# One run on 64x64 tiles in place of two: values, scores and sums of an attention block put together

## The chip, the cores and the metric

One core of a Trainium2 chip. The metric is the device time of one execution in microseconds (us). Engines are named as in the profile: PE (TensorE matmul), PEld (its weight loads), DVE (VectorE), ACT (ScalarE), POOL (GpSimd), SP (SyncE, which issues most DMAs).

## The reference, cut to what matters

Chunked attention (8 batches, 8 heads, 576 tokens, chunks of 64, head size 64) is followed by a bilinear feed-forward layer on 4608 tokens:

```python
scores = scale * np.matmul(q_c, k_c.transpose(0, 1, 2, 4, 3))   # 64x64 per chunk and head
attn = np.exp(scores - np.max(scores, axis=-1, keepdims=True))
attn = attn / (np.sum(attn, axis=-1, keepdims=True) + 1e-09)
out = np.matmul(attn, v_c)            # ... reordered to x, 4608 x 512
a = x @ w_a                           # 512 -> 1536
b = x @ w_b
return (a * b @ w_out)                # 1536 -> 512
```

## The kernel before

The tokens are cut into 9 blocks (0 to 8) of 512, a block into two units of 256. Attention of a unit has four steps: `scores` (32 matmuls on 64x64 tiles of the PE array, then two exp on ACT), `sums` (4 matmuls of 512 columns against ones, also on 64x64 tiles, then two ln on ACT), `inverse` (exp of minus ln, on ACT) and `values` (32 matmuls on 64x64 tiles, then two products on DVE).

```python
    def sums(U, halves=None):
        E = E_of[U]
        sm = [bank() for _ in range(2)]
        for cl in range(2):
            for j in range(2):
                nc.tensor.matmul(
                    sm[cl][j * 64:j * 64 + 64, :],
                    ones[cl * 64:cl * 64 + 64, :],
                    E[cl * 64:cl * 64 + 64, j].rearrange("p m g s -> p (m g s)"),
                    start=True,
                    stop=True,
                )
        ...
        for cl in range(2):
            nc.scalar.activation(
                out=ln_of[U][:, cl].rearrange("p m n -> p (m n)"), in_=sm[cl], func=AF.Ln
            )
```

From block 2 on the feed-forward layer runs in 6 groups to a block. Each group is seven half-size products, `p1` to `p7`, of four 128x128 matmuls of 256 columns, with evictions and additions between. The PSUM bank `B` of a group is one of two (`pb0`, `pb1`), taken in turn; and `p3` of a group is done one group later, after that group's `p1`.

```python
        def p1(self):
            self.A = bank(psum_a)
            self.product(self.A, self.b11, self.x11, True)
            self.B = bank(psum_b)                      # psum_b[0], then the two change places
            nc.scalar.copy(out=self.B, in_=self.A)
        ...
        def add7(self):
            self.c = c_pool.tile([128, 512], FP32, name="c_sb")
            nc.vector.tensor_tensor(out=self.c, in0=self.C, in1=self.v, op=ADD)
            nc.vector.tensor_tensor(out=self.C, in0=self.C, in1=self.u, op=ADD)

        def p3(self):
            self.product(self.B, self.b22, self.s4)
            self.multiply(self.B, self.b, 0)           # DVE reads B

        def p4(self):
            self.product(self.C, self.t4, self.x22)
            self.multiply(self.C, self.c, 256)         # DVE reads C
```

`combine_x` makes four sums of x for these products on DVE. The attention steps are put between the products: `at(K, i, n, f, u)` means that in block K, group i, place n, step f is done for unit u. `bring` casts a unit on POOL, loads the next and transposes q and k by DMA; `chunk` does parts of the output product.

```python
        def scores_beside(pool):
            return lambda u: scores(u, (pool, psum_b[0]), 1)

        for K in range(2, NBLK):
            U = 2 * K + 2
            ...
                at(K, 0, 0, sums, U)
            at(K, 1, 0, inverse, U)
            at(K, 2, 1, values, U)
            at(K, 2, 1, scores_beside(psum_o), U + 1)
            at(K, 3, 0, sums, U + 1)
            at(K, 3, 1, inverse, U + 1)
            at(K, 4, 1, values, U + 1)
            at(K, 4, 1, scores_beside(psum_q), U + 2)
            at(K, 5, 0, lambda u: combine_x(u // 2, (0,)), U + 1)
            at(K, 5, 1, lambda u: combine_x(u // 2, (1,)), U + 1)
        ...
                now = Group(K, i)
                now.p1()
                if last:
                    last.add7()
                chunk(chunks.get(K, chunks[4])[2 * i])
                ...
                if last:
                    last.p3()
                attend(K, i, 0)                        # place 0
                now.p6()
                if last:
                    last.p4()
                    finish(last)                       # sums of the products, on POOL
                ...
                now.p2()
                chunk(chunks.get(K, chunks[4])[2 * i + 1])
                attend(K, i, 1)                        # place 1
                now.p5()
                exps()
                now.p7()
                last = now
```

The softmax here doesn't subtract the row's maximum and nothing guards it: scores larger than these inputs give would overflow.

Of the kernel before, what the change touches and what calls it, by code (L numbers as in the profile page):

```python
# [16 lines left out]
def kernel(  # L17
# [10 lines left out]
    nc = tc.nc  # L28
    BF16 = mybir.dt.bfloat16
    FP32 = mybir.dt.float32  # L30
    AF = mybir.ActivationFunctionType
# [32 lines left out]
    psum_a = ctx.enter_context(tc.tile_pool(name="psuma", bufs=1, space=PSUM))  # L64
# [3 lines left out]
    psum_c = ctx.enter_context(tc.tile_pool(name="psumc", bufs=1, space=PSUM))  # L68
    psum_o = ctx.enter_context(tc.tile_pool(name="psumo", bufs=1, space=PSUM))
    psum_q = ctx.enter_context(tc.tile_pool(name="psumq", bufs=1, space=PSUM))  # L70
# [17 lines left out]
    def bank(pool=None):  # L88
        if pool is None:
            pool = spread[0]  # L90
            spread.append(spread.pop(0))
        if pool is psum_b:
            pool = psum_b[0]
            psum_b.append(psum_b.pop(0))
        return pool.tile([128, 512], FP32, name=bank_names[id(pool)])
# [97 lines left out]
    def load(U, names="qkv"):  # L193

        for n in names if U < NU else "":
            src = {"q": q, "k": k, "v": v}[n]
            if U < PE_UNITS[n]:
                st = st_pool.tile([128, H, 2, D], FP32, name="st")
                for r, b, s, m in pieces(U):
                    nc.sync.dma_start(  # L200
                        out=st[r // 2:(r + m) // 2].rearrange("p h i d -> p h (i d)"),
                        in_=src[b, :, s:s + m, :].rearrange("h (p i) d -> p h (i d)", i=2),
                    )
                staged[n, U] = st.rearrange("p h i d -> p i h d")
            else:
                staged[n, U] = st_pool.tile([128, 2, H, D], FP32, name="st")
                load_natural(staged[n, U], src, U)
# [3 lines left out]
    def cast(U, names="qkv"):  # L211
        for n in names if U < NU else "":
            if U >= 4 and wo_sums:
                combine_wo(*wo_sums.pop(0))
            raw[n, U] = raw_pool.tile(
                [128, 2, H, D], BF16, name=f"{n}_raw"
            )
            eng = nc.vector if U == 0 and n != "v" else nc.gpsimd
            eng.tensor_copy(out=raw[n, U], in_=staged.pop((n, U)))  # L219
# [28 lines left out]
    def transpose_dma(U):  # L248
        if U not in qkt:
            qkt[U] = qkt_pool.tile([128, 2, 2, NKT, 128], BF16, name="qkt")  # L250
        for w, n in ((0, "q"), (1, "k")):
            if U < PE_UNITS[n]:
                continue
            nc.sync.dma_start_transpose(
                out=qkt[U][:, w].rearrange("p g m c -> p (g m) c"),
                in_=raw.pop((n, U)).rearrange("p g h d -> p (g h d)"),
            )
# [3 lines left out]
    ln_of = {}  # L261
# [29 lines left out]
    def exps(n=2):  # L291
        while late and n:
            late.pop(0)()
            n -= 1

    def sums(U, halves=None):
        E = E_of[U]
        sm = [bank() for _ in range(2)]
        for cl in range(2):
            for j in range(2):  # L300
                nc.tensor.matmul(  # L301
# [5 lines that stand above are left out]
                )  # L307
        ln_of[U] = sm_pool.tile([128, 2, NKT, 128], FP32, name="ln")
        rs_of[U] = ln_of[U]
        for cl in range(2):  # L310
            nc.scalar.activation(
                out=ln_of[U][:, cl].rearrange("p m n -> p (m n)"), in_=sm[cl], func=AF.Ln
            )
            if halves:
                inverse(U, cl)

# [43 lines left out]
        if f is not None:  # L360
            values(f)

    def bring(U):

        if U >= NU:
            return
        cast(U, "qk")
        load(U + 1, "q" if U < 9 else "qkv")
        transpose_dma(U)
        bring_v(U)  # L370

    def bring_v(U):
        cast(U, "v")
        if U < 9:
            load(U + 1, "kv")
# [36 lines left out]
    def combine_x(K, parts=(0, 1, 2, 3)):  # L412
        xT = x_tiles[K]
        x11, x12 = xT[:, 0:2, 0:256], xT[:, 2:4, 0:256]
        x21, x22 = xT[:, 0:2, 256:512], xT[:, 2:4, 256:512]
        if K not in s_of:
            s_of[K] = [s_pool.tile([128, 2, 256], FP16, name=f"s{j}") for j in range(1, 5)]
        s1, s2, s3, s4 = s_of[K]
        for part in parts:
            o, x0, x1, op = (  # L420
                (s1, x21, x22, ADD),
                (s2, s1, x11, SUB),
                (s3, x11, x21, SUB),
                (s4, x12, s2, SUB),
            )[part]
            nc.vector.tensor_tensor(out=o, in0=x0, in1=x1, op=op)
# [245 lines left out]
    with tc.manual_schedule(  # L672
# [95 lines left out]
        def chunk(n=1):  # L768
            for _ in range(min(n, len(outs))):
                outs.pop(0)()  # L770
# [11 lines left out]
        halves = [(ft, u) for u in range(2) for ft in range(NFT)]  # L782
# [64 lines left out]
        def at(K, i, n, f, u):  # L847
            if u < NU:
                attention.setdefault((K, i, n), []).append(lambda: f(u))

        def scores_beside(pool):
            return lambda u: scores(u, (pool, psum_b[0]), 1)

        for K in range(2, NBLK):
            U = 2 * K + 2
            if K == 2:
                at(K, 0, 0, lambda u: combine_x(2, (2, 3)), U)
                at(K, 0, 0, scores, U)
                at(K, 0, 1, sums, U)
            else:  # L860
                attention[K, 0, 0] = [lambda K=K: combine_x(K, (2,))]
                attention[K, 0, 1] = [lambda K=K: combine_x(K, (3,))]
                at(K, 0, 0, sums, U)
            at(K, 1, 0, inverse, U)
            at(K, 2, 1, values, U)
            at(K, 2, 1, scores_beside(psum_o), U + 1)
            at(K, 3, 0, sums, U + 1)
            at(K, 3, 1, inverse, U + 1)
            at(K, 4, 1, values, U + 1)
            at(K, 4, 1, scores_beside(psum_q), U + 2)  # L870
            at(K, 5, 0, lambda u: combine_x(u // 2, (0,)), U + 1)
            at(K, 5, 1, lambda u: combine_x(u // 2, (1,)), U + 1)

        def attend(K, i, n):
            for f in attention.get((K, i, n), ()):
                f()

        last = None
        chunks = {
            2: (1, 1, 1, 1, 1, 2, 1, 2, 3, 0, 1, 1),  # L880
            4: (1, 1, 1, 1, 2, 1, 1, 2, 2, 0, 1, 1),
            NBLK - 1: (1,) * 12,
        }

# [7 lines left out]
        for K in range(2, NBLK):  # L892
            for i in range(NWP):
                if i == (2 if K == 2 else 1):
                    for j in range(3):
                        combine_ab(K - 1, 3, j)
                if i == 1:
                    bring(2 * K + 4)
                elif i == 3 and K > 2:
                    bring(2 * K + 5)  # L900
                elif i == 3:
                    cast(9, "qk")
                    load(10)
                    transpose_dma(9)
                if i == 0:
                    g = OutGroup(K - 1)
                    outs += [
                        lambda g=g, n=n, th=th: g.part(n, th) for n in range(7) for th in range(2)
                    ]
                now = Group(K, i)  # L910
                now.p1()
                if last:
                    last.add7()
                chunk(chunks.get(K, chunks[4])[2 * i])
                if K == 2 and i == 0:
                    for j in range(3):
                        combine_wo(3, j)
                if last:
                    last.p3()
                attend(K, i, 0)  # L920
# [3 lines that stand above are left out]
                    finish(last)  # L924
                if K == 2 and i < 3:
                    combine_w(i + 3, 3)
                if K == 2 and i == 4:
                    cast(9, "v")
                now.p2()
                chunk(chunks.get(K, chunks[4])[2 * i + 1])  # L930
                attend(K, i, 1)
                now.p5()
                exps()
                now.p7()
                last = now
        ends = [
# [46 lines left out]
```

## Time and profile before

| | before |
|---|---|
| timed runs | 303.89 us median of 3 (303.74 to 304.29) |
| span of the profiled run | 758.4 us, state slow |
| busy in that profile | PE 753.7, DVE 213.3, ACT 203.8, POOL 191.4 us |
| 64x64 runs in the compiled PE order | 41 |

The only profile of before at hand when the prediction was made came from a run 2.5 times slower than the timed ones.

### The profile page before, as it was taken

The numbers are of one execution on the slowest core, as the hardware profiler recorded it, in microseconds if no ns is written. First come the engines' busy times: TensorE is split into PE (matmuls) and PEld (weight loads), VectorE is DVE, ScalarE is ACT, GpSimd is POOL, SyncE is SP. The second block draws the span as 40 slices with busy tenths as digits, with TensorE's granted clock in tenths as the row PEclk, the third lists the DMA queues.
The fourth block names the chain that finished last, engine by engine and source line by source line (L and its number), as shares of the span: only waits on it lengthen the run. The fifth ranks groups of instructions, "written<-read, shape, count | busy, mean of one in ns | idle before, by whom it ended". The sixth has DMA issues, their size and how long they took to land.

```text
span 758.4 us, 8609 instructions
## 1 busy us (share of the span) xinstructions
PE 753.7 (99%) x3527; PEld 410.6 (54%) x3527; DVE 213.3 (28%) x343; ACT 203.8 (27%) x355; POOL 191.4 (25%) x180
## 2 busy tenths in 40 slices
PE   9999999999999999999999999999999999999998
PEld 4223455444555555565656555555555555555555
DVE  3233222133222312242223222232233223322221
ACT  4112231132332232223232323232322232222211
POOL 4674200057101260036003510251014001310220
DMA  9997220052800253014401450043011000000011
GB/s 296 321 324 160 59 48 1 14 119 70 187 1 28 73 122 56 29 53 107 91 1 41 116 122 1 29 111 56 1 29 28 1 1 29 28 1 0 1 55 55
DMA packets 141159, 54.29 MB, mean 72 GB/s; under 512 B 117184, under 2 KB 135232, under 8 KB 141120
## 3 DMA queue, kind: packets, MB, share of 16 engines
q1 hardware_dynamic: 140976, 53.69, 27.5%
q8 instruction: 27, 0.44, 0.2%
q14 instruction: 12, 0.10, 0.0%
q10 hardware_dynamic: 144, 0.07, 0.0%
HBM read 37.75 MB, written 9.44 MB: 62 GB/s over the span
## 4 chain that ended last, share of the span: by engine, by line
PE 99%; DVE 0%; ACT 0%; issue 0%
PE pb L446 20%; PE po L589 14%; PE pc L446 13%; PE pa L446 13%; PE pq L589 11%; PE po L396 4%; PE pc L396 4%; PE pb L396 4%; PE pb L662 3%; PE pa L396 2%; PE pq L396 2%; PE pc L101 2%; PE pt L301 1%; PE pt L334 1%; PE pt L237 1%; PE pt L589 1%
## 5 line engine op out<-in xcount | busy, mean ns | idle before, releaser
L526 POOL TENSOR_TENSOR so<-ab_sb 128x512 f16<-128x512 f16 x23 | 27.4, 1190 | 399.3 <-DVE ab_sb L496 345.6
L446 PE MATMUL pa<-xT,wb 128*128 128x256 f16 x336 | 119.8, 537 | 0.0
L446 PEld LDWEIGHTS <-t 128*128 128x128 f16 x504 | 84.5, 170 | 63.7 <-issue 5.6
L446 PE MATMUL pb<-s,wa 128*128 128x256 f16 x336 | 117.7, 529 | 0.0
L589 PEld LDWEIGHTS <-ab_sb 128*128 128x128 f16 x390 | 68.4, 176 | 47.1 <-issue 0.5
L446 PEld LDWEIGHTS <-wb 128*128 128x128 f16 x336 | 58.9, 175 | 42.1 <-issue 1.0
L446 PEld LDWEIGHTS <-wa 128*128 128x128 f16 x336 | 55.6, 169 | 38.5 <-issue 1.0
L589 PEld LDWEIGHTS <-so 128*128 128x128 f16 x288 | 50.4, 175 | 34.5
L496 DVE SCALAR_TENSOR_TENSOR ab_sb<-pb,b_sb 128x512 f16<-128x512 f32 x42 | 29.1, 692 | 135.1 <-PE pb L446 135.1
L484 DVE TENSOR_TENSOR c_sb<-pc,v_sb 128x512 f32<-128x512 f32 x42 | 29.0, 691 | 122.3 <-PE pc L446 96.5
L446 PE MATMUL pc<-xT,t 128*128 128x256 f16 x168 | 60.1, 538 | 0.0
L446 PE MATMUL pc<-s,t 128*128 128x256 f16 x168 | 60.1, 538 | 0.0
L589 PE MATMUL pq<-wo,so 128*128 128x256 f16 x180 | 59.5, 539 | 0.0
L589 PE MATMUL po<-wot,ab_sb 128*128 128x256 f16 x180 | 59.0, 539 | 0.0
L446 PE MATMUL pb<-s,t 128*128 128x256 f16 x168 | 57.7, 522 | 0.0
L589 PE MATMUL po<-wo,ab_sb 128*128 128x256 f16 x168 | 56.7, 535 | 0.0
L496 DVE SCALAR_TENSOR_TENSOR ab_sb<-pc,c_sb 128x512 f16<-128x512 f32 x42 | 29.1, 692 | 74.2 <-PE pc L446 74.2
L457 ACT COPY u_sb<-pb 128x512 f32<-128x512 f32 x42 | 24.6, 586 | 80.9 <-PE pb L446 65.4
L464 ACT COPY pb<-pa 128x512 f32<-128x512 f32 x42 | 23.9, 570 | 76.2 <-PE pa L446 76.2
L219 POOL CAST v_raw<-st 128x1024 bf16<-128x1024 f32 x18 | 19.0, 1054 | 100.5 <-PE pt L334 86.5
L457 ACT COPY b_sb<-pa 128x512 f32<-128x512 f32 x42 | 24.6, 586 | 72.2 <-PE pa L446 72.2
L396 PEld LDWEIGHTS <-wa 128*128 128x128 f16 x144 | 25.5, 177 | 32.5 <-issue 19.4
(129 smaller groups left out, 786.0 us busy)
## 6 DMA issues: line engine op xcount, KB each, us to landing
st<-in_v_dram SPq DMA_DIRECT2D x32, 256.0 KB, 4.4
out_dram<-o_sb SPq DMA_DIRECT2D x30, 256.0 KB, 2.1
st<-in_k_dram SPq DMA_DIRECT2D x22, 256.0 KB, 4.1
st<-in_q_dram SPq DMA_DIRECT2D x20, 256.0 KB, 3.5
st<-in_q_dram SPq DMA_DIRECT2D x6, 512.0 KB, 6.3
st<-in_moe_w_b_dram SPq DMA_DIRECT2D x6, 512.0 KB, 6.6
st<-in_moe_w_a_dram SPq DMA_DIRECT2D x6, 512.0 KB, 6.4
st<-in_moe_w_out_dram SPq DMA_DIRECT2D x6, 512.0 KB, 6.9
```

Of the source, the lines that this page charges most:

```text
L101: nc.tensor.matmul(t, warm_in[:, :128], warm_in, start=True, stop=True)
L219: eng.tensor_copy(out=raw[n, U], in_=staged.pop((n, U)))
L237: nc.tensor.transpose(tp[i][:, m, :], src[:, i, 2 * m:2 * m + 2, :].rearrange("p j d -> p (j d)"), identity,)
L396: nc.tensor.matmul(ps[n], w_ab[n, i][:, kt, o:o + 128], xT[:, kt, c0:c1], start=(kt == 0), stop=(kt == NKT - 1),)
L446: nc.tensor.matmul(t[:, h * 256:h * 256 + 256], w[:, kt, h * 128:h * 128 + 128], x[:, kt], start=start and h == 0 and kt == 0, stop=h == 1 ...
L457: nc.scalar.copy(out=t, in_=src)
L464: nc.scalar.copy(out=self.B, in_=self.A)
L484: nc.vector.tensor_tensor(out=self.c, in0=self.C, in1=self.v, op=ADD)
L496: nc.vector.scalar_tensor_tensor(out=self.dst[:, :, c0:c0 + 256], in0=t.rearrange("p (h n) -> p h n", h=2), scalar=AB_SCALE, in1=o.rearran ...
L526: (eng or nc.gpsimd).tensor_tensor(out=o, in0=x0, in1=x1, op=op)
L589: nc.tensor.matmul(t[:, c0:c0 + 256][:, cols], a[:, kt, th * 128:th * 128 + 128], w[:, kt, cols], start=n in (0, 4) and first and kt == 0, ...
L662: nc.tensor.matmul(out_ps[K, tg], ab_tiles[K][:, ft, tg * 128:tg * 128 + 128], wo_sb[:, ft], start=(ft == 0), stop=(ft == NFT - 1),)
```

## The change

Each run on 64x64 tiles makes the array change from 128x128 tiles and back. From block 4 on, the change gets one unit further ahead with the scores, so that the sums of the second unit find their exponentials ready and can stand in one run with the values of the first unit and the scores of the unit two on. Of two sums steps per block one then has a run of its own.

```diff
-    def sums(U, halves=None):
+    def sums(U, halves=None, pools=(None, None)):
...
+        def sums_beside(pool):
+            return lambda u: sums(u, pools=(psum_a, pool))
...
+                if K == 4:
+                    at(K, 0, 0, scores_beside(psum_o), U + 1)
                 at(K, 0, 0, sums, U)
             at(K, 1, 0, inverse, U)
             at(K, 2, 1, values, U)
-            at(K, 2, 1, scores_beside(psum_o), U + 1)
-            at(K, 3, 0, sums, U + 1)
+            if K < 4:
+                at(K, 2, 1, scores_beside(psum_o), U + 1)
+                at(K, 3, 0, sums, U + 1)
+            else:
+                at(K, 2, 1, scores_beside(psum_c), U + 2)
+                at(K, 2, 1, sums_beside(psum_o), U + 1)
             at(K, 3, 1, inverse, U + 1)
             at(K, 4, 1, values, U + 1)
-            at(K, 4, 1, scores_beside(psum_q), U + 2)
+            at(K, 4, 1, scores_beside(psum_q), U + (2 if K < 4 else 3))
...
-            4: (1, 1, 1, 1, 2, 1, 1, 2, 2, 0, 1, 1),
+            3: (1, 1, 1, 1, 2, 1, 1, 2, 2, 0, 1, 1),
+            4: (0, 1, 1, 1, 2, (1, 1), 1, 2, 2, 0, 1, 1),
+            5: (1, 1, 1, 1, 1, (1, 1), 1, 2, 2, 0, 1, 1),
...
                 if i == 1:
-                    bring(2 * K + 4)
-                elif i == 3 and K > 2:
-                    bring(2 * K + 5)
+                    bring(2 * K + 4 if K < 4 else 2 * K + 5, "qkv" if K < 4 else "qk")
+                elif i == 3 and K == 3:
+                    bring(11)
                 elif i == 3:
-                    cast(9, "qk")
-                    load(10)
-                    transpose_dma(9)
+                    bring(9, "qk") if K == 2 else cast(2 * K + 5, "v")
+                elif i == 5 and K > 2:
+                    bring(2 * K + 6)
```

Left out: the second ln of a joint run is queued and issued after the next group's `p1`, and in group 2 one output part moves behind `p5`.

More of the change, by code (lines that the diff above doesn't have):

```diff
@@ L294, in exps @@
             n -= 1
-    def sums(U, halves=None):
+    late_ln = []
+    def sums(U, halves=None, pools=(None, None)):
         E = E_of[U]
-        sm = [bank() for _ in range(2)]
+        sm = [bank(p) for p in pools]
         for cl in range(2):
@@ L309, in sums @@
         rs_of[U] = ln_of[U]
+        ln = ln_of[U]
         for cl in range(2):
-            nc.scalar.activation(
-                out=ln_of[U][:, cl].rearrange("p m n -> p (m n)"), in_=sm[cl], func=AF.Ln
-            )
+            late_ln.append(
+                lambda cl=cl: nc.scalar.activation(
+                    out=ln[:, cl].rearrange("p m n -> p (m n)"), in_=sm[cl], func=AF.Ln
+                )
+            )
+        for cl in range(1 if pools[0] else 2):
+            late_ln.pop(0)()
             if halves:
@@ L361, in slot, with bring @@
             values(f)
-    def bring(U):
+    def bring(U, names="qkv"):
         if U >= NU:
@@ L369, in bring @@
         transpose_dma(U)
-        bring_v(U)
+        if "v" in names:
+            bring_v(U)
     def bring_v(U):
@@ L907 @@
                     outs += [
-                        lambda g=g, n=n, th=th: g.part(n, th) for n in range(7) for th in range(2)
-                    ]
+                        lambda g=g, n=n, th=th: g.part(n, th)
+                        for n in range(7)
+                        for th in range(2)
+                    ]
+                steps = chunks.get(K, chunks[5])[2 * i:2 * i + 2]
+                c0, c1, c2 = steps[0], *(steps[1] if type(steps[1]) is tuple else (steps[1], 0))
                 now = Group(K, i)
                 now.p1()
+                while late_ln:
+                    late_ln.pop(0)()
                 if last:
                     last.add7()
-                chunk(chunks.get(K, chunks[4])[2 * i])
+                chunk(c0)
                 if K == 2 and i == 0:
@@ L929 @@
                 now.p2()
-                chunk(chunks.get(K, chunks[4])[2 * i + 1])
+                chunk(c1)
                 attend(K, i, 1)
@@ L933 @@
                 exps()
+                chunk(c2)
                 now.p7()
```

## The prediction

> **What bounds the kernel now.** I read, in this order: the list of cores, busy times and slices on the page, the chain that ended last, PE's own waits, and the timeline of PE and ACT around the steps that the change moves. The first view warns about all the others:
>
> ```profile
> core 0: 758.4 us, clock 1.000
> ```
>
> The timed runs took 303.74 to 304.29 us; the profiled one spans 758.4, 2.50 times the 303.89, and is marked slow, although its recorded clock is 1.000. So the profile gives the order of the work and true durations of the other engines, but a slowed PE, and too much slack everywhere else.
>
> ```profile
> PE 753.7 (99%) x3527; PEld 410.6 (54%) x3527; DVE 213.3 (28%) x343; ACT 203.8 (27%) x355; POOL 191.4 (25%) x180
> ...
> PE  9999999999999999999999999999999999999998
> ...
> PE 99%; DVE 0%; ACT 0%; issue 0%
> ```
>
> PE is full in every slice and is 99% of the chain. Set against 303.89 us the others would be busy 70% (DVE), 67% (ACT) and 63% (POOL): none is the bound, but each is near enough to make a local wait that this profile cannot show. PE's own waits come to 1.7 us, at the two ends:
>
> ```profile
> PE pc L101 <- DVE warm_in L80: 1.3, 1, 1.3
> PE pa L589 <- DVE o_sb L598: 0.4, 1, 0.4
> ```
>
> The steps that the change regroups, in block 5 (values, then scores, which run on to 454.10; then the separate sums step):
>
> ```profile
> 451.02 2.03 PE L589 MATMUL pq<-wo,so 128*128 128x256 f16 x6
> 452.98 0.69 PE L334 MATMUL pt<-E,v_raw 64*64 64x64 bf16 x32
> ...
> 454.10 1.31 PE L446 MATMUL pb<-s,wa 128*128 128x256 f16 x4
> 455.24 1.41 PE L446 MATMUL pc<-s,t 128*128 128x256 f16 x4
> ...
> 459.31 1.41 PE L446 MATMUL pb<-s,wa 128*128 128x256 f16 x4
> 460.65 0.69 PE L301 MATMUL pt<-E,ones 64*64 64x512 bf16 x4
> 461.27 1.31 PE L446 MATMUL pb<-s,t 128*128 128x256 f16 x4
> 462.28 1.16 PE L446 MATMUL pc<-xT,t 128*128 128x256 f16 x3
> ```
>
> The columns are start, length, engine, line, operation. Read the starts: the modelled lengths overlap. Two 64x64 runs stand here 6.5 us apart, and each makes the array change from 128x128 to 64x64 and back.
>
> **What the Trainium skill says.** "TensorE: Matmul & The Clock Gate", section "Back-to-back issue gap", gives N/2.4 + 2.5 ns per warm matmul: 109 ns at 256 columns, 216 at 512. This trace does not agree: starts of neighbouring 256-column matmuls lie a mean of 295 ns apart (242 to 379), 2.7 times as much. For the timed runs the trace's rate is impossible: some 2040 such matmuls x 295 ns would be 602 us. So for those I use the page's gap, as an estimate. "TensorEngine Tiling (Array Packing)", section "Key Properties", says that changing the tiling mode drains the TensorE. The trace agrees in part: the last big matmul before a 64x64 run is followed by a start about 472 ns later, not 295. But the big matmuls just after the run start closer than usual, so that little is lost in all: from 459.31 to 462.28 is 2.97 us for eight 256-column matmuls (8 x 0.295 = 2.36) and the sums, whose four 512-column matmuls stand side by side and cost one pass (0.216 x 2.7 = 0.58), 2.94 together. Whatever slows PE in this profile also hides the drains. "TensorE: Matmul & The Clock Gate", section "Single matmul latency", gives (398 + N)/2.4 ns for one that nothing overlaps: 272 ns at 256, 379 at 512, so that a drain exposes about 163 ns beyond the gap. No line here shows that number at full clock.
>
> **The change part by part.**
>
> 1. Arithmetic: none added or removed. Both kernels have 7056 rows on PE, 3527 of them matmuls, and 326 on DVE. ACT goes from 340 to 344 rows and the sync queue from 105 to 108; they are lists split in other places, not more evictions.
>
> 2. Array mode changes: counting in the compiled PE order how often matmuls on 64x64 tiles are interrupted by full ones gives 41 runs before, 37 after. From block 4 each block had four: sums of the first unit; values + scores; sums of the second unit; values + scores. It now has three: sums; values + scores + sums; values + scores. Block 4 takes the additional scores, needed to get one unit ahead, into the run of its first sums. So four sums steps (blocks 4 to 7), at 382, 461, 539 and 618 us of the profile, lose their own entry and exit: 8 mode changes. At 163 ns each this is 8 x 0.163 = 1.30 us, all on PE, hence on the path that sets the end.
>
> A check by budget, an estimate too: PE's 753.7 us divided by 2.7 are 280 us of array work. The timed 303.9 leave 24. About 3 us are the tail after the last matmul (755.4 to 758.4 in the profile) and some 7 the start, where data must arrive. The remaining 14 over 41 runs are 0.34 us a run, near the 0.33 of two drains. If some of these 14 us are waits instead, a run is worth less. The low side is the visible entry alone, 472 - 295 = 177 ns, of the slowed trace, divided by 2.7: 0.07 us a run, 0.3 us in all.
>
> 3. Evictions on ACT. The joint run fills pc and pb0 or pb1 with scores and pa and po with sums, instead of po and pb, and later two pt. The first exp and the first ln follow at once, the second of each later. No operation is added, the order is denser.
>
> ```profile
> 455.44 0.59 ACT L457 COPY v_sb<-pb 128x512 f32<-128x512 f32 x1 [0.63 <-PE pb L446]
> 455.92 0.60 ACT L285 ACTIVATE E<-pb 128x512 bf16<-128x512 f32 x1
> ```
>
> Two evictions one behind the other start 0.48 us apart. After the joint run ACT has E, ln, v, E and the copy of pa to pb. By hand, from the end of the run: E, ln at once to 1.0 us; v needs p5 (0.44 us) and ends at about 1.5; E at 2.0. PE does p5, an output part (0.66), p7 and the next p1, 4 x 109 ns for each of the products: 1.97 us. So pa's copy ends near 2.6 and p6, which needs it, comes after another output part and p3, at 3.1. Margin 0.5 us: no wait. The split of the output parts around p5 is what gives this margin.
>
> 4. POOL and loads. Casts of unit 2K+6 move to the last group of the block before (i = 5), ahead of that group's combinations. 3 casts x about 1.05 us put these 3 us later. Their reader, the third output product, comes in group 2 of the next block. A group takes about (168 + 84) x 0.109 / 6 = 4.6 us, so casts and the six combinations (3.2 + 6 x 1.16 = 10.1 us, starting about half a group into i = 5) end before it. The transposes (2.8 and 2.9 us to landing) have three groups, 14 us. Expected cost: 0.
>
> Sum: 303.89 - 1.30, with nothing to add, is 302.6 us.
>
> **The rivals.** (a) *The drains cost nothing here*: the slowed trace, taken at its word, shows 2.97 against 2.94 us. Against it stands the budget's 24 us. It would make 303.9. (b) *ACT becomes a local wait*: PE's next p1 waits for pa, or p6 for the copy. My margin is 0.5 us on hand-worked starts; were it missed by 0.5 us in each of three or four runs, the gain would go: 303.9 to 304.5. For it speaks ACT's 67%; against it that an average block does not get more work. (c) *POOL is late*: the output products wait for the combinations that the casts delay; 1 us a block in three blocks would make 305. In the profile POOL idled 345.6 us for PE's results, slack that shrinks at full speed, yet it stays at 63%. (d) *The removed steps also waited*: at full speed the separate sums may have waited for the second exp, or for pt. Then each merge saves 0.2 to 0.5 us more: 301 to 302. Nothing in the slowed profile can show it; by the same hand count the second exp was done about 0.5 us before the old sums.
>
> **Range and chances.** Centre 302.6. From (a) and a little of (b) the top is 303.9, from (d) the bottom 301.2. To leave 2% it must go below 297.8 or above 310.0; the first would need 6.1 us, 1.5 us for each removed run, as long as six 512-column passes, the second a new wait of 1 us or more in every late group. I put faster at 0.02, same at 0.97, slower at 0.01.
>
> **What would show it.** In the changed kernel's trace: 37 runs, sums following scores with no big matmul between, no entry gap between them; pa, po and pc read by ACT within about 2 us of the run; no PE wait for ACT, DVE or POOL. If its profile is slowed too, its span should hardly move (under 1 us), since the slowing hides drains, while the timed runs gain about 1.3. The prediction is wrong if the timed gain is under 0.3 or over 2.7 us, or if PE waits appear at p1, p6 or the output products.

## The result and the profile after

| | before | after |
|---|---|---|
| timed runs of the same rounds | 303.99 us median of 4 (303.74 to 304.29) | 305.13 us median of 4 (304.65 to 305.62) |
| ratio | 1 | 1.0037, 95% interval 1.0018 to 1.0056 |

Ratios here and below are the mean time of one kernel's fast runs over that of the other's of the same rounds, so not quite the ratio of the medians. The change is within 2%, and slower by about 1.1 us, where 1.3 us less was predicted. That the change would stay within 2% was right; the direction was not.

This time the profiled run was a fast one. Its page, cut to the lines that answer to those of before, and its waits of PE:

```profile
PE 292.5 (96%) x3527; PEld 232.4 (77%) x3527; DVE 211.2 (70%) x343; ACT 196.5 (65%) x355; POOL 194.8 (64%) x180
...
PE   6799999999999999998999999999999999999995
...
PE 85%; DVE 6%; ACT 3%; DMA 2%; issue 1%; SPq 1%; POOL 0%; DVEq 0%; ACTq 0%
```

```profile
PE pc L101 <- DVE warm_in L80: 1.3, 1, 1.3
PE pb L274 <- DVE ab_sb L504: 1.1, 1, 1.1
...
PE pc L454 <- DVE ab_sb L504: 0.6, 3, 0.2
```

PE is still the bound, but two waits stand here that before's slowed profile could not show. The first is the digit 8 in PE's slices: scores (L274) wait once for DVE's product out of a bank `pb`, of the PSUM memory that PE writes to. The timeline of PE and then of DVE at that place, the first group of block 4 (columns: start, length, engine, line, operation, and in brackets idle time and what ended it):

```profile
141.06 0.60 PE L454 MATMUL pb<-s,wa 128*128 128x256 f16 x4
...
142.95 0.22 PE L274 MATMUL pb<-qkt 64*64 64x64 bf16 x2 [1.15 <-DVE ab_sb L504]
```

```profile
141.02 0.68 DVE L492 TENSOR_TENSOR c_sb<-pc,v_sb 128x512 f32<-128x512 f32 x1
141.62 0.68 DVE L493 TENSOR_TENSOR pc<-pc,u_sb 128x512 f32<-128x512 f32 x1
142.22 0.68 DVE L504 SCALAR_TENSOR_TENSOR ab_sb<-pb,b_sb 128x512 f16<-128x512 f32 x1
```

At 141.06 PE does `p3` of the group before into that group's `B`. The additional scores of block 4 come right after it, and `psum_b[0]`, the bank that `scores_beside` takes, is at place 0 this same `B`: `p1` has just turned the two. At place 1, where all other scores stand, DVE has long read it. Here DVE has two additions to do first, and then the product that frees the bank, which ends at 142.90. From PE's starts, the matmul into `pb` comes 1.36 us after the one before it; side by side they normally start a few ns apart.

The second wait is smaller and comes twice, at `p7` in group 5 of blocks 4 and 5. (The third of its line stands at the end of block 2, where the trace of before, `e1_before_again`, has one too.) The timeline of all engines there, cut to DVE, POOL and the waiting product:

```profile
169.34 0.69 DVE L504 SCALAR_TENSOR_TENSOR ab_sb<-pb,b_sb 128x512 f16<-128x512 f32 x1
169.95 1.03 POOL L219 CAST q_raw<-st 128x1024 bf16<-128x1024 f32 x1
169.95 1.31 DVE L434 TENSOR_TENSOR s<-xT 128x512 f16<-128x512 f16 x1
...
171.19 0.68 DVE L504 SCALAR_TENSOR_TENSOR ab_sb<-pc,c_sb 128x512 f16<-128x512 f32 x1
...
171.92 0.60 PE L454 MATMUL pc<-s,t 128*128 128x256 f16 x4 [0.21 <-DVE ab_sb L504]
```

DVE's sum of x starts together with a POOL cast and takes 1.31 us; it is over about 0.3 us after the cast. So the product out of `pc` is late, and `p7`, which writes `pc` anew, starts 483 ns after the matmul before it instead of 109. This wait is 0.37 us a time.

### The profile page after: what moved, and what is told of

The parts are those of the page before. It is cut to its first block, busy times and chain, and to the rows that moved or that the text cites. A ratio compares the mean times of both kernels' runs of the same rounds, so it can differ in the third digit from the quotient of the medians.

```text
span 303.2 us, 8609 instructions
## 1 busy us (share of the span) xinstructions
PE 292.5 (96%) x3527; PEld 232.4 (77%) x3527; DVE 211.2 (70%) x343; ACT 196.5 (65%) x355; POOL 194.8 (64%) x180
## 4 chain that ended last, share of the span: by engine, by line
PE 85%; DVE 6%; ACT 3%; DMA 2%; issue 1%; SPq 1%; POOL 0%; DVEq 0%; ACTq 0%
PE pb L454 17%; PE pc L454 12%; PE pa L454 11%; PE po L597 11%; PE pq L597 10%; PE po L404 3%; PE pc L404 3%; PE pb L404 3%; PE pb L670 3%; DMA st<-in_k_dram 2%; PE pa L404 2%; PE pq L404 2%; PE pt L341 2%; DVE s L434 1%; PE pt L303 1%
## 5 line engine op out<-in xcount | busy, mean ns | idle before, releaser
L454 PEld LDWEIGHTS <-t 128*128 128x128 f16 x504 | 48.6, 98 | 8.8 <-issue 2.8
L454 PE MATMUL pb<-s,wa 128*128 128x256 f16 x336 | 50.5, 273 | 0.0
L454 PE MATMUL pa<-xT,wb 128*128 128x256 f16 x336 | 50.4, 273 | 0.0
L597 PEld LDWEIGHTS <-ab_sb 128*128 128x128 f16 x390 | 37.8, 98 | 5.2 <-issue 0.9
L454 PEld LDWEIGHTS <-wa 128*128 128x128 f16 x336 | 31.8, 98 | 5.0 <-issue 1.1
L493 DVE TENSOR_TENSOR pc<-pc,u_sb 128x512 f32<-128x512 f32 x42 | 28.9, 689 | 0.0
L534 POOL TENSOR_TENSOR so<-so,ab_sb 128x512 f16<-128x512 f16 x23 | 26.8, 1166 | 1.7
L534 POOL TENSOR_TENSOR ab_sb<-ab_sb 128x512 f16<-128x512 f16 x23 | 27.1, 1179 | 0.0
L454 PE MATMUL pc<-s,t 128*128 128x256 f16 x168 | 25.2, 272 | 0.6 <-DVE ab_sb L504 0.6
L454 PE MATMUL pc<-xT,t 128*128 128x256 f16 x168 | 25.2, 272 | 0.1
```

What stands on the lines that cost most here:

```text
L454: nc.tensor.matmul(t[:, h * 256:h * 256 + 256], w[:, kt, h * 128:h * 128 + 128], x[:, kt], start=start and h == 0 and kt == 0, stop=h == 1 ...
L534: (eng or nc.gpsimd).tensor_tensor(out=o, in0=x0, in1=x1, op=op)
L597: nc.tensor.matmul(t[:, c0:c0 + 256][:, cols], a[:, kt, th * 128:th * 128 + 128], w[:, kt, cols], start=n in (0, 4) and first and kt == 0, ...
```

## The experiments

Three sets, each on one chip with its own runs of before. Three causes could explain a loss in place of a gain: theory A, the bank in block 4; theory B, later narrowed to C, the new order of casts and loads (C: a cast that holds DVE); or a third, that the merging itself gains nothing.

**First set.** Before: 303.56 us median (11 runs). Experiment `e1_before_again` has no edit.

> The kernel before once more, unchanged, to get a profile in the fast state (the one at hand was slowed 2.5 times) and a control. Both theories: time ratio to before 1.000 within 0.002. If its profile is fast: 41 runs on 64x64 tiles; a separate sums step should take about 545 ns from the last full matmul before it to the first after it (as the sums steps that the changed kernel keeps), a values+scores run about 872 ns; no PE wait of about 1.1 us at block 4. Theory A (one bank wait in block 4 eats the gain): stretch of blocks 5 to 7 is longer than in the changed kernel by about 3 x 0.19 us. Theory B (the other order of casts, loads and output parts costs): blocks 5 to 7 are no longer here than in the changed kernel.

Measured: 303.63 us, ratio 1.001 (0.9988 to 1.0032). The profile is fast; it shows 40 runs, as two matmul records near the start are missing (3525 of 3527). Its timeline of PE at the separate sums step of block 5, and then that of the changed kernel at the joint run of the same block (cut: the lines of the scores, after the values in both, and the later lines of the sums):

```profile
184.49 0.82 PE L589 MATMUL pq<-wo,so 128*128 128x256 f16 x6
185.24 0.45 PE L334 MATMUL pt<-E,v_raw 64*64 64x64 bf16 x32
185.91 0.61 PE L446 MATMUL pb<-s,wa 128*128 128x256 f16 x4
...
187.88 0.60 PE L446 MATMUL pb<-s,wa 128*128 128x256 f16 x4
188.41 0.41 PE L301 MATMUL pt<-E,ones 64*64 64x512 bf16 x4
188.75 0.61 PE L446 MATMUL pb<-s,t 128*128 128x256 f16 x4
```

```profile
184.37 0.82 PE L597 MATMUL pq<-wot,so 128*128 128x256 f16 x6
185.12 0.45 PE L341 MATMUL pt<-E,v_raw 64*64 64x64 bf16 x32
185.68 0.41 PE L303 MATMUL pa<-E,ones 64*64 64x512 bf16 x2
...
186.03 0.61 PE L454 MATMUL pb<-s,wa 128*128 128x256 f16 x4
```

Read starts again. Before: values and scores 185.24 to 185.91, 0.67 us; sums 188.41 to 188.75, 0.34. After: 185.12 to 186.03, 0.91 for all three. Exact starts give the price of a run: the first 64x64 matmul starts 202 ns after the last of 256 columns, 93 more than the gap of 109; the first big one starts 118 to 125 ns after the last of 64 columns and 333 after the last of 512, about 90 and 117 more than streaming takes. A separate sums step lengthens PE's work by 545 - 109 = 436 ns, sums inside a run by 1117 - 872 = 245 (a joint run takes 1116 or 1117 ns from the last full matmul before it to the first after it, the usual values-and-scores run 871 or 872). So a merge saves 0.19 us, and four save 0.76.

Summing in both traces, from 78 us to the end, what each start-to-start distance has beyond streaming (N/2.4 + 2.5 ns; inside the runs, distances over 60 ns) gives the difference:

| extra time on PE, us | before (`e1_before_again`) | after |
|---|---|---|
| entries to 64x64 runs | 2.33 (25) | 1.96 (21) |
| exits from them | 2.58 | 2.17 |
| waits inside such runs | 0.27 | 1.42 |
| waits and excess between big matmuls | 2.08 | 2.72 |
| sum | 7.26 | 8.27 |

The merging wins 0.78 us, the waits inside runs cost 1.15 more, those between products 0.64: 1.0 us in all, against 1.1 in the timed runs. The sum starts at 78 us because this run of before, the slowest of its six, lost 1.2 us earlier in a wait for a POOL cast of `wa`; so the two profiled spans, 303.3 and 303.2 us, are alike.

The expectation named a test by stretches. From the first product of block 5 to that of block 8 it took 89.69 us here and 89.06 in the changed kernel: longer by 0.63, as theory A has it and theory B does not. About 0.29 of this is the scores of unit 17, which the changed kernel does earlier (a run of values alone takes 580 ns, with scores 872). Block 4 took 30.04 us here and 31.73 in the changed kernel: the loss lies there.

**`e2_banks_oq`** mends the bank of block 4 alone. Bank `pq` is free there:

```diff
-                    at(K, 0, 0, scores_beside(psum_o), U + 1)
+                    at(K, 0, 0, lambda u: scores(u, (psum_o, psum_q), 1), U + 1)
```

> The changed kernel, but the additional scores of block 4 go to banks po and pq instead of po and the next of the two pb banks, which the product p3 just before has written and DVE still has to read. Theory A: the wait of 1.15 us for DVE there is gone, and the time falls by 1.0 to 1.3 us against the changed kernel, to about 303.9 (ratio to before 0.998 to 1.001). Theory B: the wait was absorbed later (ACT or DVE would have held PE anyway) or is not what matters, and the time stays within 0.4 us of 305.1 (ratio about 1.003).

Measured: 303.12 us, ratio 0.9992 (0.9964 to 1.002). The wait for DVE is gone, but the profiled run, at 305.55 the slowest of the six, had another at the same place:

```profile
PE po L274 <- DMA qkt<-k_raw: 1.4, 1, 1.4
...
PE pb L454 <- ACT v_sb L465: 0.7, 1, 0.7
```

Unit 11's scores stand 2.5 groups earlier than before the change, but its DMA transposes do not: SP issued that of k at 140.90 us here, at 135.94 in the changed kernel's own trace. The second line belongs to block 3: there PE's matmuls started 0.90 and 0.41 us late, the first behind an ACT that had waited 2.27 us for a store of outputs. So DMA was late in this run before the edited place was reached, and the run's extra time is not that of one wait. The other five runs were 302.47 to 303.54. So the bank matters as theory A says, and the early use of unit 11 leaves little room; this single reading doesn't show how often that costs. The fall against the changed kernel is one between different sets; it stands on the ratios to before, 0.9992 and 1.0037.

**`e3_bring_only`** takes the kernel before with only the new order of casts, loads and transposes.

```diff
                 if i == 1:
-                    bring(2 * K + 4)
-                elif i == 3 and K > 2:
-                    bring(2 * K + 5)
+                    bring(2 * K + 4 if K < 4 else 2 * K + 5, "qkv" if K < 4 else "qk")
+                elif i == 3 and K == 3:
+                    bring(11)
                 elif i == 3:
                     ...
+                elif i == 5 and K > 2:
+                    bring(2 * K + 6)
```

> The kernel before with only the changed order of casts, loads and DMA transposes (unit 2K+6 brought in group 5 of block K, unit 2K+5 in group 1, its v cast in group 3); runs on 64x64 tiles, banks and output parts as before. Theory A: no effect, ratio to before 1.000 within 0.001 (304.0). Theory B: this order makes POOL late or disturbs DVE, and the time rises by 0.6 to 1.2 us (ratio 1.002 to 1.004).

Measured: 303.93 us, ratio 1.001 (0.9994 to 1.0025). By time alone this is inconclusive. Its trace has one wait of 0.38 us at `p7` in group 5 of block 5, with DVE's sum at 1.24 us beside a cast that had begun 78 ns earlier; in block 4 it has none. So such waits come with this order without any merging, but not in every block: too little for all of the loss.

**Second set**, on another chip. Before: 304.06 us (11 runs). `e4_after_again` is the changed kernel, as the base.

> The changed kernel once more, as the common base of this set. From its first trace: merged steps win 4 x 0.19 us, block 4 loses 1.36 us inside the scores (bank pb still to be read by DVE), and two products p7 in group 5 of blocks 4 and 5 lose 0.37 us each. Expected ratio to before 1.002 to 1.004 (304.2 to 304.8 if before is at 303.6).

Measured: 305.49 us (304.66 to 307.62), ratio 1.0062 (1.0036 to 1.0088), more than expected. The trace has the same waits as the first: 1.36 us in block 4, 0.37 twice at `p7`.

**`e5_casts_apart`** moves the casts away from DVE's sums in group 5:

```diff
-                elif i == 5 and K > 2:
-                    bring(2 * K + 6)
+                elif i == 4 and K > 2:
+                    bring(2 * K + 6, "qk")
...
                     finish(last)
+                if i == 5 and K > 2:
+                    cast(2 * K + 6, "v")
```

> The changed kernel with the casts of q and k of unit 2K+6 in group 4 instead of 5, and the cast of v after group 5's first combinations; banks as changed. Theory C (a POOL cast that starts together with DVE's two-input sum in group 5 holds it for the whole cast, and p7 waits 0.37 us): these waits vanish, 0.4 to 0.7 us are gained on the changed kernel. Rival (the waits come and go with run-to-run timing whatever stands there, and are hidden later): within 0.2 us of the changed kernel. The wait of 1.36 us in block 4 stays in both.

Measured: 304.56 us (303.65 to 306.95), ratio 1.0026 (0.9998 to 1.0054), 0.9 us below the run before it, which by time alone is not clear of noise. Both waits at `p7` are gone from the trace. But the wait in block 4 has grown, by PE's starts from 1.36 to 1.86 us:

```profile
PE pb L274 <- DVE ab_sb L504: 1.6, 1, 1.6
```

DVE reached block 4 later there, after a sum of x that took 1.00 us beside POOL. The trace thus gives the edit 2 x 0.37 - 0.50, about 0.25 us of the 0.9. A further 0.36 us lies in block 2, which the edit doesn't touch; the rest is within the spread of these two kernels' runs.

**`e6_casts_and_banks`** has both edits, of `e2_banks_oq` and `e5_casts_apart`.

> As the run before it, and the additional scores of block 4 in banks po and pq. If both causes are right and add up, 1.4 to 2.0 us faster than the changed kernel, 302.8 to 303.1 (ratio to before 0.997 to 0.998), the 0.76 us of the merged steps being what is left. Rival: block 4 then waits for the DMA transpose of unit 11 instead (the last profile with these banks showed 1.5 us of it), and only half of that comes.

Measured: 302.76 us (302.36 to 303.43), ratio 0.9966 (0.9953 to 0.9979): 1.8 us below the run before it, as much as the wait there, and 2.7 below the changed kernel, more than the expected 1.4 to 2.0. It beats both kernels. The same stretch of group 5 in its timeline, cut as above:

```profile
167.86 0.69 DVE L504 SCALAR_TENSOR_TENSOR ab_sb<-pb,b_sb 128x512 f16<-128x512 f32 x1
168.47 0.42 DVE L434 TENSOR_TENSOR s<-xT 128x512 f16<-128x512 f16 x1
168.80 0.69 DVE L504 SCALAR_TENSOR_TENSOR ab_sb<-pc,c_sb 128x512 f16<-128x512 f32 x1
169.56 1.15 POOL L534 TENSOR_TENSOR so<-ab_sb 128x512 f16<-128x512 f16 x1 [1.04 <-DVE ab_sb L504]
```

POOL's instruction before ends 57 ns into DVE's sum, and then POOL is idle; the sum takes 0.42 us instead of 1.31.

**`e7_sums_apart`** undoes the merging alone, all else as in `e6_casts_and_banks`:

```diff
-                at(K, 2, 1, sums_beside(psum_o), U + 1)
+                at(K, 3, 0, sums, U + 1)
```

> As the run before it, but the second unit's sums stand apart again, in group 3 and in the two pt banks: the merging alone undone, all else kept. If a run on 64x64 tiles costs 0.195 us (94 ns on entry, about 90 to 100 on exit), this is 4 x 0.195 = 0.78 us slower than the run before it. With the 0.33 us a run that the prediction used it would be 1.3 us slower. Rival (merging itself gains nothing in time, as ACT's denser order gives it back): within 0.2 us.

Measured: 303.89 us (303.55 to 304.62), ratio 1.0004 (0.9991 to 1.0017). That is 1.1 us slower than the run before it. The spread of the six runs of each leaves about 0.6 to 1.7 us, so the time shows that the merging gains, but doesn't decide between 0.78 and 1.3. The traces do: entries and exits differ by 0.77 us, as expected. `e7_sums_apart` has 0.34 us more of other excess, mainly two waits at `p7` and `p4` where block 3 passes into block 4 (0.31 and 0.28 us), ahead of the first step that was set apart, so not an effect of the merging.

**Third set**, on a third chip. Before: 303.50 us (11 runs). It repeats two kernels unchanged.

> The changed kernel with the block 4 banks alone mended, again, as its first profile was a slow run with a wait of 1.5 us for the DMA transpose of unit 11. If that wait is a matter of single runs, this profile lacks it and the time is 0.997 to 0.999 of before, with 0 to 2 waits of 0.37 us at p7 in group 5. If the wait is regular, it shows again and the ratio is 1.000 or above.

> The version with both mendings again, on another draw of chip: 0.9955 to 0.998 of before if the result holds, and 0.2 to 0.7 us below the run ahead of it, by the waits at p7 that the casts cause. Rival (what was measured was one chip's luck): ratio 0.999 to 1.001.

Measured: `e8_banks_again` 303.07 us (302.70 to 304.20), ratio 0.9992 (0.9977 to 1.0007), with no wait for the transpose in its trace, so that wait does not come in every run, and one wait of 0.38 us at `p7` in block 5; its ratio is just above the range expected for that case. `e9_best_again` 302.37 us (5 runs, 302.33 to 303.46), ratio 0.997 (0.9957 to 0.9984): the gain holds on another chip. The casts' part is 0.7 us between the medians, not quite clear of noise, of which the trace's waits at `p7` explain 0.38.

Taken over the ten profiles at full speed, the waits go with the edits. The five with these casts in group 5 (`after`, `e2_banks_oq`, `e3_bring_only`, `e4_after_again`, `e8_banks_again`) all have the wait at `p7` in block 5, 0.37 or 0.38 us; the other five have none there. In block 4 two of the five have it. And PE waits for DVE in block 4's additional scores in the three with bank `pb` there (1.36, 1.36, 1.86 us), and in none of the five with bank `pq`.

## Why the prediction was wrong

**PE as the bound, and no wait for ACT or for late POOL results: right.** PE is 85% of the chain after, and its waits list no eviction by ACT behind a joint run. The margin on ACT's side was 0.26 us and not 0.5 (block 4: the copy of `pa` ended at 158.72 us, `p6` started at 158.98), but it sufficed.

**Part 2, eight mode changes of 0.163 us: the count right, the size too large.** 37 runs instead of 41 came. A merge saves 0.19 us, not 0.33, and four 0.78 by the traces instead of 1.30. The latency of an isolated matmul, which the term was taken from, was too large a measure for a drain. The mis-sized term alone would still have left a gain of 0.78 us. The budget that seemed to confirm it (24 us beyond array work, 14 of them given to the runs) had other waits in it: PE was busy for 291.8 us of a 303.3 us span in before's fast profile, and all extra time around 64x64 runs from 78 us on was 5.2.

**The sentence in part 2 that fails: "Block 4 takes the additional scores ... into the run of its first sums".** It was counted as a run saved, and its banks were not looked at. Part 3 worked through the banks of the joint runs alone. One look at which of the two `pb` banks is first at place 0 would have shown that PE must wait there for three DVE operations, each starting about 0.6 us after the last. The wait of 1.36 us outweighs all four merges, and taking it away (`e5_casts_apart` to `e6_casts_and_banks`) gave 1.8 us back.

**Part 4, "Expected cost: 0": wrong.** It asked whether POOL's results come too late for their readers, and they do not. It did not ask what a POOL cast does to DVE. The Trainium skill says it, in "SBUF — State Buffer", section "Who interferes with whom": a DVE instruction with two SBUF inputs contends with a GpSimd instruction that reads SBUF, the shared ports are an exclusive lock, and issue order decides who blocks. The traces agree: the same sum took 0.42 us with POOL idle and 1.31 us beside a cast. It need not be a cast. In the ten profiles at full speed 42 of the 140 sums with both inputs in `xT` took about 0.42 us; the other 98 were longer and ended 277 to 286 ns after the POOL instruction, cast or combination, that ran when they began or started within 5 ns of that. In group 5 the new casts start about when the sum does, so that nearly their whole length is added to it. The mean of all 14 such sums was 753 ns in the changed kernel, 615 in before's fast profile and 596 in `e6_casts_and_banks`. The same part took 14 us as the lead of the transposes. In the changed kernel's trace the scores start 7.8 to 11.2 us after SP issued the transpose of k for units 12 to 17, and only 5.7 us after it for unit 11, at the switch in block 4.

**The rivals and the range.** (b), (c) and (d) looked for ACT, for POOL's results and for waits that the change would end; none of them is what came. That (c) names 305 us, near the measured time, is luck: no output product waited for POOL. (d) is answered by before's fast trace: its separate sums steps all take 545 ns, so none of them waited. The range ended at 303.9 because no rival had the switch from one schedule to the other in it. The statement on a slowed profile could not be tested: the profile after was fast.

## What to carry to other kernels

When a schedule shifts by one step, work through the block where it switches as carefully as the steady state: an additional step there meets banks and transfers at another place in their turn. For work that moves on POOL, ask what DVE does with two SBUF inputs at that moment, not only who reads POOL's result. And the profile of a slowed PE gave here neither the price of a drain nor the waits on other engines; get one at full speed before pricing tenths of a microsecond.

## What the Trainium skill lacked or had wrong

- "TensorEngine Tiling (Array Packing)", section "Key Properties", says that a mode change drains, with no price. Here: 93 ns on entry after a 256-column matmul, about 90 on exit after 64 columns and 117 after 512. An estimate from "TensorE: Matmul & The Clock Gate", section "Single matmul latency", was 163 ns, too much.
- "TensorE: Matmul & The Clock Gate", section "Back-to-back issue gap": the page gives N/2.4 + 2.5 ns as the gap of an isolated matmul and ~131 ns for 512 columns in a real kernel. In this stream of weight loads and matmuls the formula held (medians of 109 ns at 256 columns and 216 at 512, in before's fast trace) and 131 ns was not seen; the prediction, which used the formula, was lucky in this.
- No page that was read describes the state of the first profile: recorded clock 1.000, yet matmuls in bursts (starts 31 ns apart for four side by side, then one of about 153) that repeat every 216 ns, and a mean gap of 295 ns where the fast runs have 109. A sums step there cost 2.97 us with its neighbours where their mean pace gives 2.94.
- "SBUF — State Buffer", section "Who interferes with whom", was right, and the prediction should have used it. What the runs add is how close the race is, and that the recorded starts don't tell who wins it: in `e2_banks_oq` DVE's sum began 2 ns before a cast (at 170.89 us) and took 417 ns while the cast took 1310; in the changed kernel another that also began 2 ns before a cast (at 108.21 us) took 1316 while the cast took 1035.
